# Decode attention with a mixer: keys and values of two neighbouring heads loaded together, in rows of 64 KB

## The chip, the cores and the metric

The kernel runs on one core of one Trainium2 chip. The metric is the device time of one execution in microseconds (us); lower is better. A run of the kernel before is compared with runs of the kernel after on the same chip.

The engines are PE (TensorE, matmuls), DVE (VectorE), ACT (ScalarE), POOL (GpSimd) and SP (SyncE, which here only issues DMA transfers). Each engine works through its own instructions strictly in order. The bytes are moved by 16 DMA engines which all serve one queue of transfers that SP issues.

## What is computed

```python
B, Sq, D = 8, 1, 512
Hq, Hkv, Sk, Dh = 32, 8, 8192, 128
q = (xn @ wq).reshape(B, Sq, Hq, Dh).transpose(0, 2, 1, 3)
scores = einsum("bhqd,bhkd->bhqk", q, repeat(k_cache, 4)) * Dh ** -0.5
o = einsum("bhqk,bhkd->bhqd", softmax(scores), repeat(v_cache, 4))
attention = o.transpose(0, 2, 1, 3).reshape(B, Sq, Hq * Dh) @ wo
# mixer on the second layer norm h of x, token by token
u = gelu(einsum("bsd,sf->bdf", h, w1) + b1)          # F = 1792
return x + attention + (einsum("bdf,fs->bds", u, w2) + b2).transpose(0, 2, 1)
```

One token of 8 batch elements attends to a cache of 8192 positions, with 32 query heads on 8 heads of keys and values. Everything is float32. Keys and values of one head and one batch element are 4 MB each, 537 MB in all: the kernel reads each byte once.

## The kernel before

**Items.** The work is cut into 64 items (`N_IT`), one for each head `h` and batch element `b`, with `h, b = divmod(i, B)`. An item has K(i) and V(i) of 4 MB. Both are loaded with 128 partitions; partition p holds 64 consecutive positions, so one row is 32 KB.

**The ring.** `slots` (in the trace `raw`) is a ring of `RING = 5` slots of 4 MB. `slot()` (L49) hands them out in turn. `load_next()` (L87) takes the next load from the list `order` (K0, K1, V0, K2, V1, ...) and has SP issue it. SP waits with it until the work that last used this slot is done, and everything that SP has to issue later waits behind it. `load_next()` is called where a slot comes free: at the end of `qk(i)` for the keys, and at the end of `pv(i, 1)` for the values.

**What one item needs**, by engine:
- `turn_keys(i, c)` (L256), four times: DVE transposes a chunk of 128 x 2048 keys in place, in blocks of 32 x 32.
- `qk(i)` (L263): PE multiplies 4 blocks of 32 head dimensions with 4 chunks, 16 instructions that add up in one bank `acc`. The queries lie spread out in `z` (`Z`), which `q_place(h)` fills once for each head by matmuls of PE and copies of ACT. [...] The four chunks use four different groups of 32 columns of the array.
- The softmax: `sm_max` (DVE, L282), `sm_spread` (PE, L287, which lays the maxima of all partitions side by side), `sm_bias` (DVE, L293, the maximum over partitions with `hmask`), `sm_exp` (ACT, L304, with a table load ahead of it), `sm_send` (PE, L311, which reorders the partitions with `send`), `sm_turn` (DVE, L322, into one of two tiles `pt`).
- `pv(i, part)` (L327): PE multiplies with V, 16 instructions in two parts. `o_take` (ACT, L358) copies the result to `ob`, and `o_place` (after every fourth item) sums and scales it with `ohg`, `pick` and `keep` into `ot`. `o_project(h)` (L402) multiplies a whole head with `wo`, and `load_wo` loads the next 1 MB of `wo` afterwards.

**The order.** It is written by hand (`manual_schedule`), in `pair(i)` (L439): one turn of the loop handles three items at different stages, i the transposition of keys, i-1 the QK and softmax, i-2 the PV. The last items have an order of their own (from L493 on), and in the last fifteen turns SP also issues a tiny transfer into `pad` (L490).

**The mixer** is spread between. It has 112 pieces `mx_step(b, j)` (14 for each of 8 batch elements, two in each turn): a gelu on ACT, a product and a sum on POOL. Where one batch element ends, `mx_end(b)` (L431) has PE sum `macc` over partitions (L433) and DVE add the result to `yrow` (L434), and `mx_begin` has PE spread the next row into `hb` (L419).

Of the kernel before, what the change touches and what calls it, by code (L numbers as in the profile page):

```python
# [10 lines left out]
ALU = mybir.AluOpType  # L11
# [17 lines left out]
N_IT = B * HKV  # L29
RB = 2 * REP  # L30
# [10 lines left out]
def attn_mixer_kernel(ctx: ExitStack, tc: tile.TileContext, x, kc, vc, wq, wo, w1, b1, w2, b2, out):  # L41
# [29 lines left out]
    KR, VR = {}, {}  # L71
    order = []
    for i in range(N_IT):
        order.append((2 * i, kc, KR, i))
        order.append((2 * (i + LAG) + 1, vc, VR, i))
# [10 lines left out]

    def load_next():  # L87
        if order:
# [4 lines left out]
            first, last = to is KR and not i, not order  # L93
            at = 0
            for n in (CH_T,) * NCH if first else PIECES if last else (NT,):
                nc.sync.dma_start(t[:, at:at + n, :], rows[:, at:at + n, :])
                at += n
# [6 lines left out]
    def load_wo(h):  # L104
        t = place.tile([P, REP, D], F32, name="wo")
        how = "(r p) n -> p r n" if h == HKV - 1 else "(p r) n -> p r n"
        rows = wo[h * REP * DH:(h + 1) * REP * DH, :].rearrange(how, p=P)
# [10 lines left out]
    w1t = const.tile([P, NF], F32, name="w1t")  # L118
    b1t = const.tile([P, NF], F32, name="b1t")
    w2t = const.tile([P, NF], F32, name="w2t")  # L120
    b2t = const.tile([B, 1], F32, name="b2t")
    yrow = const.tile([W, D], F32, name="yrow")
    for _ in range(RING - 2):
        load_next()
# [12 lines left out]
    oh = early[:, 3, W:W + REP]  # L137
    nc.vector.tensor_reduce(oh, ident.rearrange("p (g h) -> p h g", h=REP), AX.X, ALU.add)
    ohw = early[:, 2, :P]
    nc.vector.tensor_copy(ohw.rearrange("p (g h) -> p g h", h=REP),  # L140
                          oh.unsqueeze(1).to_broadcast([P, P // REP, REP]))
    hmask = const.tile([P, P], F32, name="hmask")
    nc.vector.tensor_scalar(hmask, ohw, 1.0, 3.0e38, op0=ALU.subtract, op1=ALU.mult)
    oh32 = early[:, 3, :W]
    nc.vector.tensor_reduce(oh32, ident.rearrange("p (j x) -> p x j", x=W), AX.X, ALU.add)
    ohu = const.tile([P, GT * REP], F32, name="ohu")
    nc.vector.tensor_copy(ohu, oh32[:, :GT * REP])
# [8 lines left out]
    ohg = const.tile([P, P], F32, name="ohg")  # L156
    nc.vector.tensor_scalar(ohg.rearrange("p (h g) -> p h g", h=REP), oh.unsqueeze(2).to_broadcast([P, REP, W]),
                            lmask, None, op0=ALU.mult)
    send = const.tile([P, P], F32, name="send")
    nc.vector.tensor_copy(send.rearrange("p (x c h) -> p c x h", c=NCH, h=REP),  # L160
                          ident.rearrange("p (c x h) -> p c x h", c=NCH, h=REP))
# [4 lines left out]
    pick = const.tile([P, GT, P], F32, name="pick")  # L166
    nc.vector.tensor_copy(pick.rearrange("p u (h g) -> p (u h) g", h=REP),
                          ohu.unsqueeze(2).to_broadcast([P, GT * REP, W]))
    keep = const.tile([P, P], F32, name="keep")
    nc.vector.tensor_copy(keep.rearrange("p (g c) -> p g c", c=REP), oh32.unsqueeze(2).to_broadcast([P, W, REP]))  # L170
# [9 lines left out]
    Z = const.tile([P, NB, B, W], F32, name="z")  # L180
# [43 lines left out]
    def q_project():  # L224
# [16 lines left out]
        load_next()  # L241

    def q_place(h):
        m = misc()
        for q in range(NB):
            nc.tensor.matmul(m[:, q * B * REP:(q + 1) * B * REP], rep[:, q, :], QT[:, h].rearrange("p b r -> p (b r)"),
                             start=True, stop=True)
        src = m[:, :NB * B * REP].rearrange("p (x r) -> p x r", r=REP)
        dst = Z.rearrange("p q b (a k r) -> p (q b) a k r", k=2, r=REP)
        for a in range(NB):  # L250
            x = slice(a * W, (a + 1) * W)
            for k in range(2):
                nc.scalar.copy(dst[x, :, a, k, :], src[x])
# [9 lines left out]
    def qk(i, part=None):  # L263
# [4 lines left out]
        for q in range(NB):  # L268
            for c in range(NCH) if part is None else range(part * NCH // 2, (part + 1) * NCH // 2):
                nc.tensor.matmul(S[i][c * W:(c + 1) * W, :].rearrange("p (t j) -> p t j", j=W),  # L270
                                 Z[:, q, b, :], k[:, c * CH_T:(c + 1) * CH_T, q * W:(q + 1) * W],
# [37 lines left out]
    def sm_send(i):  # L309
        m = misc()  # L310
        nc.tensor.matmul(m, send, st[i][0], start=True, stop=True)  # L311
# [41 lines left out]
    def o_take(i):  # L353
# [7 lines left out]
        oc = one.tile([P, DH], F32, name=f"oc{i % 2}")  # L361
# [11 lines left out]
    def o_place(i):  # L373
# [3 lines left out]
        if h < HKV - 1:  # L377
            if b % HB < HB - 1:
                return
            ob = OB.pop(h)  # L380
            m = misc()
            nc.tensor.matmul(m[:, :HB], ohg, LR.pop(i // HB), start=True, stop=True)
            rl = work.tile([P, HB], F32, name="rl4")
            nc.vector.reciprocal(rl, m[:, :HB])
            m = misc()
            for c in range(NCH):
                nc.tensor.matmul(m.rearrange("p (b d) -> p b d", b=HB), pick[:, c, :], ob[:, :, c * DH:(c + 1) * DH],  # L387
                                 start=(c == 0), stop=(c == NCH - 1))
            t = big()
            nc.vector.tensor_tensor(t.rearrange("p (b d) -> p b d", b=HB), m.rearrange("p (b d) -> p b d", b=HB),  # L390
                                    keep.unsqueeze(1).to_broadcast([P, HB, P]), op=ALU.mult)
            s = work.tile([P, HB, REP], F32, name="s4")
            nc.vector.tensor_reduce(s, t.rearrange("p (b g c) -> p b c g", b=HB, c=REP), AX.X, ALU.add)
            o = b - HB + 1
# [187 lines left out]
```

## Time and profile before

| | us |
|---|---|
| three runs | 1294.78, 1294.83 (median), 1295.08 |
| the profiled execution | 1294.88 |
| its span, first to last instruction | 1293.1 |
| PE, DVE, ACT, POOL busy | 829.3, 726.9, 331.2, 229.6 |
| bytes moved by DMA | 554.45 MB, mean 429 GB/s |

All numbers of the trace come from the one profiled execution. Its rows are read so: in a row of the timeline stand the start, the length, the engine, the line, the operation with output and inputs, how many were merged (x), and in brackets the idle time of the engine ahead of it with what ended it. In a row of a group stand the busy time in all, the mean of one in ns, and the idle time ahead of it. In a row of stretches stand the length, the busy time of PE, PE's weight loads, DVE, ACT and POOL, then the granted clock of TensorE (1.00 is full speed), the mean busy share of the DMA engines and what they moved in GB/s. The share of a short stretch can be over 1, since a packet is counted where it begins.

### The profile page before, as it was taken

Reading aid. Unit: us, or ns where it says so; the run is one execution under the profiler, and the core shown is the slowest. Engines: PE = TensorE matmul, PEld = TensorE weight load, DVE = VectorE, ACT = ScalarE, POOL = GpSimd, SP = SyncE. Lnnn points to the kernel's source line nnn. Section 1 sums busy time; section 2 is a strip of 40 time slices with the busy share of each in tenths; the row PEclk is TensorE's granted clock in tenths of the full one; section 3 lists DMA queues with packets and bytes.
Section 4 is the critical chain, followed back from the end, with each engine's and each line's share of the span. In section 5 each row is a group of like instructions: output and inputs, shape, how many; then the busy total and the mean of one; then the engine's idle time right before and its main releaser. Section 6 shows DMA issues by size and latency. Waiting matters only on the chain.

```text
span 1293.1 us, 11759 instructions
## 1 busy us (share of the span) xinstructions
PE 829.3 (64%) x4890; PEld 244.5 (19%) x4890; DVE 726.9 (56%) x648; ACT 331.2 (26%) x479; POOL 229.6 (18%) x247
## 2 busy tenths in 40 slices
PE   2664766756757656666657576567564774657777
PEld 0111211211211111211112111121121221112223
DVE  2655456565555554654646556556456555556774
ACT  0232323222422313223233132232323232311000
POOL 1112112211212122121121131211211221110000
PEclk9877778878878788787887797787876887878899
DMA  9999999999999999999999999999999999999997
GB/s 407 426 432 436 430 435 432 432 432 434 431 432 433 433 432 431 436 431 430 434 431 433 433 430 435 431 433 433 432 431 431 435 432 428 435 432 430 433 437 315
DMA packets 21640, 554.45 MB, mean 429 GB/s; under 512 B 2732, under 2 KB 2764, under 8 KB 3540
## 3 DMA queue, kind: packets, MB, share of 16 engines
q1 hardware_dynamic: 21444, 553.68, 99.4%
q8 instruction: 38, 0.62, 0.2%
q14 instruction: 14, 0.11, 0.0%
q0 software_dynamic: 128, 0.02, 0.0%
q10 hardware_dynamic: 16, 0.02, 0.0%
HBM read 553.69 MB, written 0.02 MB: 428 GB/s over the span
## 4 chain that ended last, share of the span: by engine, by line
DMA 66%; PE 19%; DVE 14%; issue 1%; ACT 0%; SPq 0%; POOL 0%; ACTq 0%; DVEq 0%; POOLq 0%
DMA raw<-in_A_k_cache_dram 63%; PE acc L337 13%; DVE raw L259 12%; DMA raw<-in_A_v_cache_dram 2%; PE misc L287 2%; DMA b2t<-in_B_b_dram 2%; DVE mr L282 1%; PE acc L270 1%; PE misc L230 1%; PE misc L433 0%; PE misc L387 0%; PE hb L419 0%; PE misc L311 0%; DVE oc L366 0%; PE misc L218 0%
## 5 line engine op out<-in xcount | busy, mean ns | idle before, releaser
L259 DVE STREAM_TRANSPOSE raw<-raw 128x2048 f32<-128x2048 f32 x256 | 583.6, 2295 | 292.1 <-DMA raw<-in_A_k_cache_dram 292.1
L337 PE MATMUL acc<-raw,pt 128*32 128x512 f32 x2016 | 340.2, 829 | 0.0
L287 PE MATMUL misc<-ident,mr 128*128 128x128 f32 x128 | 47.0, 466 | 401.0 <-DVE mr L282 401.0
L270 PE MATMUL acc<-raw,z 128*32 128x512 f32 x2048 | 261.0, 609 | 9.7 <-DVE raw L259 7.6
L428 POOL TENSOR_SCALAR g<-g,w2t 128x512 f32<-128x512 f32 x112 | 77.7, 694 | 789.7 <-ACT g L427 789.7
L304 ACT ACT_TABLE_LOAD x57 | 73.1, 1283 | 333.8 <-DVE nb L293 333.5
L429 POOL TENSOR_TENSOR macc<-macc,g 128x512 f32<-128x512 f32 x112 | 142.3, 1271 | 9.4
L427 ACT ACTIVATE g<-hb,b1t,w1t 128x512 f32<-128x512 f32 x112 | 87.1, 777 | 219.7 <-PE hb L419 127.1
L322 DVE STREAM_TRANSPOSE pt<-misc 128x512 f32<-128x512 f32 x64 | 45.5, 710 | 140.0 <-PE misc L311 140.0
L337 PEld LDWEIGHTS acc<-raw,pt 128*32 128x32 f32 x2016 | 74.9, 145 | 211.5 <-issue 210.3
L287 PEld LDWEIGHTS misc<-ident,mr 128*128 128x128 f32 x128 | 29.4, 285 | 449.3 <-DVE mr L282 449.3
L304 ACT ACTIVATE t2k<-acc,nb 128x512 f32<-128x512 f32 x64 | 44.0, 688 | 233.4 <-DVE nb L293 232.8
L270 PEld LDWEIGHTS acc<-raw,z 128*32 128x32 f32 x2048 | 66.5, 111 | 186.3 <-issue 169.7
L311 PE MATMUL misc<-t2k,send 128*128 128x512 f32 x128 | 76.0, 677 | 23.4 <-ACT t2k L304 23.4
L427 ACT ACT_TABLE_LOAD x57 | 73.1, 1283 | 1.0
L358 ACT COPY ob<-acc 128x512 f32<-128x512 f32 x56 | 32.7, 584 | 98.9 <-PE acc L337 98.9
L387 PE MATMUL misc<-ob,pick 128*128 128x512 f32 x112 | 51.5, 603 | 0.0
L282 DVE TENSOR_REDUCE mr<-acc 128x1 f32<-128x512 f32 x64 | 41.8, 653 | 3.0 <-PE acc L270 3.0
L311 PEld LDWEIGHTS misc<-t2k,send 128*128 128x128 f32 x128 | 19.4, 191 | 78.4 <-issue 40.7
L434 DVE TENSOR_TENSOR yrow<-misc,yrow 32x512 f32<-32x512 f32 x8 | 5.4, 678 | 42.7 <-PE misc L433 42.7
L405 PE MATMUL misc<-wo,ot 128*32 128x512 f32 x56 | 27.0, 629 | 0.0
L421 POOL MEMSET macc<- 128x512 f32 x8 | 4.2, 525 | 116.4 <-PE misc L433 97.2
(90 smaller groups left out, 229.5 us busy)
## 6 DMA issues: line engine op xcount, KB each, us to landing
raw<-in_A_k_cache_dram SPq DMA_DIRECT2D x63, 4096.0 KB
raw<-in_A_v_cache_dram SPq DMA_DIRECT2D x63, 4096.0 KB
wo<-in_A_wo_dram SPq DMA_DIRECT2D x7, 1024.0 KB
raw<-in_A_k_cache_dram SPq DMA_DIRECT2D x4, 1024.0 KB
raw<-in_A_v_cache_dram SPq DMA_DIRECT2D x3, 1024.0 KB
raw<-in_A_v_cache_dram SPq DMA_DIRECT2D x2, 512.0 KB
wo<-in_A_wo_dram SPq DMA_DIRECT2D x4, 256.0 KB
ob<-in_A_x_dram ACTq DMA_DIRECT2D x1, 16.0 KB
```

Source lines behind the costliest of these rows:

```text
L259: nc.vector.transpose(k, k)
L270: nc.tensor.matmul(S[i][c * W:(c + 1) * W, :].rearrange("p (t j) -> p t j", j=W), Z[:, q, b, :], k[:, c * CH_T:(c + 1) * CH_T, q * W:(q + ...
L282: nc.vector.tensor_reduce(mr, S[i], AX.X, ALU.max)
L287: nc.tensor.matmul(m[:, :P], st[i].to_broadcast([P, P]), ident, start=True, stop=True)
L304: nc.scalar.activation(p, S.pop(i), AF.Exp, bias=st[i], scale=SCALE, accum_out=lr)
L311: nc.tensor.matmul(m, send, st[i][0], start=True, stop=True)
L322: nc.vector.transpose(PT[i % NPT][:, :CH_T * W], st.pop(i)[0])
L337: nc.tensor.matmul(O[i][j * W:(j + 1) * W, :].rearrange("p (c d) -> p c d", c=NCH), pt[:, t * W:(t + 1) * W], v[:, t], start=(t < NB), sto ...
L387: nc.tensor.matmul(m.rearrange("p (b d) -> p b d", b=HB), pick[:, c, :], ob[:, :, c * DH:(c + 1) * DH], start=(c == 0), stop=(c == NCH - 1))
L427: nc.scalar.activation(g, hb, AF.Gelu_apprx_tanh, bias=b1t[:, j:j + 1], scale=w1t[:, j:j + 1])
L428: nc.gpsimd.tensor_scalar(g, g, w2t[:, j:j + 1], 1.0, op0=ALU.mult, op1=ALU.mult)
L429: nc.gpsimd.tensor_add(acc, acc, g)
```

## The change

The first six heads (`PAIRED = 6`) are handled two at a time, in 24 steps (`N_PR`), one for each pair of heads `g` and batch element `b`. The last two heads stay with `pair(i)`, whose loop now starts at item `FIRST = 48`.

**Loads.** The keys of two neighbouring heads lie behind each other in DRAM. One load of 8 MB takes both: the first head in partitions 0 to 63, the second in 64 to 127, with 128 consecutive positions (64 KB) in each partition. It takes two neighbouring slots of the ring. Where only the last slot of the ring is left before it wraps, which is so for every fifth load, it becomes two loads of 4 MB and rows of 32 KB (V0, K3, V5, K8, V10, K13, V15, K18, V20, K23). The order is K0, V0, K1, V1, ...; in step i K(i+1) is issued after the first half of K(i), and V(i+1) after the first half of V(i).

**The step.** Its keys are transposed in eight chunks and multiplied in four quarters of two chunks, all of which add up in one bank (`Z` is wider by four columns, and the two halves take it at different offsets). Then there is one softmax for both heads, with one exponential and two sends, and the PV in two halves. The steps do not overlap as the items did: transposition, QK, softmax and PV of one step follow each other in the order of the program. Four pieces of the mixer (`mix(1)`) stand behind the four quarters.

**The rest.** The masks `hmask`, `send`, `ohg`, `pick` and `keep` exist in two forms: `fill_softmax(True, ...)` and `fill_place(True, ...)` write those for pairs at the start, and the calls with `False` in `pair(48)` write the others. Three small vectors moved into `pad`; the fifteen tiny transfers of the last turns are gone.

```diff
+    duo = [(src, to, i) for i in range(N_PR) for src, to in ((kc, KP), (vc, VP))][::-1]
+
+    def load_duo():
+        src, to, i = duo.pop()
+        g, b = divmod(i, B)
+        rows = src[b, 2 * g:2 * g + 2].rearrange("h (p t) d -> (h p) (t d)", p=HP)
+        half = NT * DH
+        if taken[0] % RING < RING - 1:
+            t = slot(2).rearrange("p s m -> p (s m)")
+            n = 1 if to is VP or i else 4
+            for a in range(n):
+                x = slice(a * 2 * half // n, (a + 1) * 2 * half // n)
+                nc.sync.dma_start(t[:, x], rows[:, x])
+            parts = [t[:, k * half:(k + 1) * half] for k in range(2)]
+        else:
+            parts = []
+            for k in range(2):
+                t = slot().rearrange("p s m -> p (s m)")
+                nc.sync.dma_start(t, rows[:, k * half:(k + 1) * half])
+                parts.append(t)
...
     def load_next():
-        if order:
+        if duo:
+            load_duo()
+        elif order:
...
+    def qk_duo(i, k, cs):
...
+        for q in range(NB):
+            for c in cs:
+                nc.tensor.matmul(SD[i][c * W:(c + 1) * W, :].rearrange("p (t j) -> p t j", j=W),
+                                 Z[:, q, b, (1 - k) * REP:(1 - k) * REP + W],
+                                 t[:, c * CH_T:(c + 1) * CH_T, q * W:(q + 1) * W],
+                                 start=(not k and not q), stop=(k == 1 and q == NB - 1))
+
+    def softmax_duo(i):
...
+        nc.vector.tensor_reduce(mr, s, AX.X, ALU.max)
+        m = misc()
+        nc.tensor.matmul(m[:, :P], mr.to_broadcast([P, P]), ident, start=True, stop=True)
...
+        nc.scalar.activation(p, s, AF.Exp, bias=nb, scale=SCALE, accum_out=LD[i // HB][:, b % HB:b % HB + 1])
+        for k in range(2):
+            m = misc()
+            nc.tensor.matmul(m, send[:, k, :], p, start=True, stop=True)
+            nc.vector.transpose(PT[k][:, :CH_T * W], m)
...
+    def mix(n):
+        for _ in range(n):
+            b, j = divmod(step[0], NF)
+            step[0] += 1
+            if j == 0 and 0 < b <= B:
+                mx_end(b - 1)
+            if b < B:
+                if j == 0:
+                    mx_begin(b)
+                mx_step(b, j)
...
+    def duo_step(i):
+        g, b = divmod(i, B)
+        half = NCH // 2
+        for k in range(2):
+            for x in range(2):
+                for c in range(half):
+                    turn_duo(i, k * NCH + x * half + c)
+                qk_duo(i, k, range(x * half, (x + 1) * half))
+                mix(1)
+            if not k:
+                load_next()
+                if i == N_PR - 1:
+                    load_next()
+        if i == N_PR - 1:
+            load_next()
+        del KP[i]
+        softmax_duo(i)
+        if b == B - 1 and g < PAIRED // 2 - 1:
+            q_place_duo(g + 1)
+        pv_duo(i, 0)
+        load_next()
+        if i:
+            place_duo(i - 1)
...
+        pv_duo(i, 1)
+        if i == N_PR - 1:
+            load_next()
+        del VP[i]
+        take_duo(i)
...
-    spare = pad[:16, :60].rearrange("p (n k) -> p n k", k=4)
-    for i in range(N_IT - 2):
+    for i in range(FIRST, N_IT - 2):
         pair(i)
-        n = N_IT - 3 - i
-        if 0 < n < 16:
-            nc.sync.dma_start(spare[:n, n - 1, :], wo[:n, :4])
```

What this does to the order of the instructions shows at the places where the mixer passes from one batch element to the next. On PE this was so before, in the turn that has the QK of item 7, the last of the first head (L270 is QK, L246 `q_place`, L287 and L311 the softmax, L337 the PV, L433 `mx_end`, L419 `mx_begin`):

```order
L270 MATMUL acc<-raw,z 32x512 x16
L246 MATMUL misc<-qt,rep 128x32 x4
L287 MATMUL misc<-ident,mr 128x128
L337 MATMUL acc<-raw,pt_146 32x512 x8
L433 MATMUL misc<-macc,bsel 32x512
L419 MATMUL hb<-hn,ident 128x512
L337 MATMUL acc<-raw,pt_146 32x512 x8
L311 MATMUL misc<-t2k,send 128x512
```

And this is PE now in step 7, where the mixer passes to its third element (L491 is `qk_duo`, L580 `mx_end`, L566 `mx_begin`, L502 and L511 the softmax, L328 `q_place_duo`, L523 `pv_duo`):

```order
L491 MATMUL acc<-raw,z 32x512 x8
L580 MATMUL misc<-macc,bsel 32x512
L566 MATMUL hb<-hn,ident 128x512
L491 MATMUL acc<-raw,z 32x512 x24
L502 MATMUL misc<-ident,mr 128x128
L511 MATMUL misc<-t2k,send 128x512 x2
L328 MATMUL misc<-qt,rep 64x32 x8
L523 MATMUL acc<-raw,pt_156 32x512 x16
L523 MATMUL acc<-raw,pt_158 32x512 x16
```

The matmul of `mx_end` stood between two halves of the PV of an earlier item; now it stands between the first and the second quarter of the step's QK, and the PV of the same step comes after the whole QK, the softmax and the two sends.

On DVE the same place read so before (L259 is the transposition of a chunk of keys, L282 and L293 the softmax, L434 the addition of `mx_end`, L322 the transposition into `pt`):

```order
L259 STREAM_TRANSPOSE raw<-raw 128x2048 x2
L282 TENSOR_REDUCE mr<-acc 128x1
L434 TENSOR_TENSOR yrow<-misc,yrow 32x512
L259 STREAM_TRANSPOSE raw<-raw 128x2048
L293 ISA t2k,nb<-misc,hmask 128x128
L293 ISA nb 128x1
L259 STREAM_TRANSPOSE raw<-raw 128x2048
L322 STREAM_TRANSPOSE pt_148<-misc 128x512
```

And now, in step 7 (L480 is the transposition of keys, L581 the addition, L500 and L504 the softmax, L512 the transpositions into `pt`):

```order
L480 STREAM_TRANSPOSE raw<-raw 128x2048 x2
L581 TENSOR_TENSOR yrow<-misc,yrow 32x512
L480 STREAM_TRANSPOSE raw<-raw 128x2048 x6
L500 TENSOR_REDUCE mr<-acc 128x1
L504 ISA t2k,nb<-misc,hmask 128x128
L504 ISA nb 128x1
L512 STREAM_TRANSPOSE pt_156<-misc 128x512
L512 STREAM_TRANSPOSE pt_158<-misc 128x512
```

The addition stood between the maximum of an item and the transposition of the third chunk of keys of the next item; now it stands between the second and the third of eight transpositions of keys whose QK, softmax and PV all come later in the same step.

More of the change, by code (lines that the diff above doesn't have):

```diff
@@ L29 @@
 N_IT = B * HKV
+PAIRED = 6
+N_PR = PAIRED // 2 * B
+FIRST = PAIRED * B
+ZW = W + REP
 RB = 2 * REP
@@ L92, in load_next @@
             rows = src[b, h].rearrange("(p t) d -> p t d", p=P)
-            first, last = to is KR and not i, not order
+            last = not order
             at = 0
-            for n in (CH_T,) * NCH if first else PIECES if last else (NT,):
+            for n in PIECES if last else (NT,):
                 nc.sync.dma_start(t[:, at:at + n, :], rows[:, at:at + n, :])
@@ L310, in sm_send @@
         m = misc()
-        nc.tensor.matmul(m, send, st[i][0], start=True, stop=True)
+        nc.tensor.matmul(m, send[:, 0, :], st[i][0], start=True, stop=True)
         st[i] = (m, st[i][1])
@@ new lines, in attn_mixer_kernel, with pv_duo @@
+    LD, OD, OBD = {}, {}, {}
+    def pv_duo(i, k):
+        b = i % B
+        if not k:
+            OD[i] = ps_a.tile([P, 512], F32, name="acc")
+        v = VP[i][k].rearrange("p (c t) d -> p t c d", c=NCH)
+        for t in range(CH_T):
+            j = t % NB
+            nc.tensor.matmul(OD[i][j * W:(j + 1) * W, :].rearrange("p (c d) -> p c d", c=NCH),
+                             PT[k][:, t * W:(t + 1) * W], v[:, t],
+                             start=(not k and t < NB), stop=(k == 1 and t >= CH_T - NB))
@@ L477, in pair @@
             sm_turn(k)
-        if mixing:
-            mx_step(mb, mj + 1)
-        if b == 3 and h:
+        if step[0] <= B * NF:
+            mix(1)
+        if h == PAIRED and b == 1:
+            o_project(h - 2)
+            load_wo(h - 1)
+        if b == 3:
             o_project(h - 1)
```

233 lines of the change are left out of this document (160 added, 73 removed).

## The prediction

> **What bounds the kernel now.** I read the stretches of the trace first: for each stretch its length, the busy time of five engines (with counts), the granted TensorE clock, the busy share of the DMA engines and GB/s.
>
> ```profile
> 60.00:1200.00 1140.00, 727.67 (x4190) 211.06 (x4186) 637.97 (x535) 315.61 (x447) 220.27 (x228) 0.80 1.00 432
> 7.35:17.07 9.72, 0.61 (x4) 0.55 (x4) 4.55 (x19) 0.59 (x2) 0.00 (x0) 1.00 1.00 433
> ```
>
> From 60 to 1200 us the DMA engines are busy all the time (1.00) at 432 GB/s, while the busiest engine, PE, works 728 of 1140 us. A load of one head (4.19 MB) therefore takes 9.7 us, the pair's load (8.39 MB) 19.4 us, and nothing on an engine counts unless it lets this queue run dry. So the next view is the chain that ended last, which shows how far ahead of its need a load is issued.
>
> ```profile
> 133.41 28.95 DMA raw<-in_A_k_cache_dram
> 174.43 26.67 DMA raw<-in_A_k_cache_dram
> ```
>
> A K load lands 26.7 to 29.0 us after its issue, of which its own bytes need 9.7: the queue holds 17 to 19 us of other work when it is issued. That is the reserve of before: an engine's delay of 10 us costs nothing. The wait that releases such an issue is mostly PV, as the waits of the DMA queue show (us in total, times, longest).
>
> ```profile
> SPq L96 <- PE acc L337: 828.4, 61, 20.8
> ```
>
> **What the change can gain.** (1) The rows. The 7.35 to 17.07 us stretch holds only the load of wq, whose rows are 64 KB like the new ones: 433 GB/s against 432 with 32 KB rows. The 48 pair loads last 48 x 19.4 = 931 us; by the two rows the gain is 0.23%, 2.1 us, but 432 is a mean with small loads in it, so the bounds are 0 and 2.1 and I take 1. The Trainium skill (DMA: Bandwidth & Descriptors, "Why small descriptors are slow") gives each packet a fixed cost of about 3 cycles on top of one cycle per 32 bytes; by that rule half as many packets would save 3 of 2054 cycles, an estimate of 1.4 us, and the sum would be 0.4 us lower. (2) Fewer small transfers and one maximum, bias and exponential for two heads: all beside a saturated queue, 0. What hides them is the DMA time itself. (3) The setup has some 20 more small DVE operations, and the masks are filled again at the seventh head. The first lie ahead of a wait for b2t,
>
> ```profile
> 23.10 0.47 DVE L210 TENSOR_SCALAR macc<-ob,b2t 8x512 f32<-8x512 f32 x1 [10.20 <-DMA b2t<-in_B_b_dram]
> ```
>
> which leaves 10.2 us of cover; the second (about 3 us of DVE) stand where 4 MB loads again lie in the queue: 0. Without that cover they would cost these 3 us once.
>
> **What it can lose.** The ring still has five slots of 4 MB, but a load now takes two. In step i K(i+1) may be issued when the first half of K(i) is multiplied (the second half of V(i-1) is by then), V(i+1) when the first half of V(i) is, which stands behind the whole softmax of step i. I set time 0 at the first transposition of K(i), which comes when K(i) has landed. V(i) lands at 19.4, K(i+1) at 38.8. The queue stays full only if K(i+1) is issued a lead before 19.4 and V(i+1) a lead before 38.8. The lead (from issue to landing without the bytes) is bounded by the one small transfer that finds the queue empty:
>
> ```profile
> 1290.06 0.66 SPq L553 DMA_DIRECT2D out_dram<-macc  x1
> SPq L578 <- DMA out_dram<-macc: 1.1, 1, 1.1
> ```
>
> 1.8 us (0.66 and 1.1) at least, 3.0 (to the end of the span at 1293.1) at most; I take 2.4. So the deadlines are 17.0 and 36.4. Now the chain of an ordinary step, with these rows (start, us, engine, line, operation, idle before):
>
> ```profile
> 162.37 4.50 DVE L259 STREAM_TRANSPOSE raw<-raw 128x2048 f32<-128x2048 f32 x2 [3.39 <-DMA raw<-in_A_k_cache_dram]
> 1263.12 3.63 PE L270 MATMUL acc<-raw,z 128*32 128x512 f32 x16
> 1261.99 0.65 DVE L282 TENSOR_REDUCE mr<-acc 128x1 f32<-128x512 f32 x1
> 1262.70 0.49 PE L287 MATMUL misc<-ident,mr 128*128 128x128 f32 x2 [1.34 <-DVE mr L282]
> 169.59 0.25 DVE L293 CUSTOM_DVE_ANT_0 t2k<-misc,hmask 128x128 f32<-128x128 f32 x1
> 169.94 1.28 ACT L304 ACT_TABLE_LOAD   x1 [7.00 <-DVE nb L293]
> 171.82 0.19 ACT L304 ACTIVATION_READ_ACCUMULATOR t2k<-acc,nb 128x1 f32 x1
> 174.28 1.12 PE L311 MATMUL misc<-t2k,send 128*128 128x512 f32 x2
> 56.29 2.08 PE L311 MATMUL misc<-t2k,send 128*128 128x512 f32 x2 [3.02 <-ACT t2k L304]
> 1248.36 1.92 PE L337 MATMUL acc<-raw,pt 128*32 128x512 f32 x16
> 150.93 6.24 PE L337 MATMUL acc<-raw,pt 128*32 128x512 f32 x32
> 54.00:58.00 4.00, 1.71 (x2) 0.50 (x2) 2.31 (x3) 3.88 (x6) 1.96 (x2) 0.50 0.97 418
> ```
>
> - Eight transpositions at 2.25 end at 4.5, 9.0, 13.5 and 18.0 by pairs. QK comes in quarters of two chunks each (8 instructions, 16 in the trace): 3.63 at full clock, as the same shape in the tail shows, no less than the whole four chunks take, since two chunks fill only half of the array's columns.
> - After 3 us of idleness PE has a granted clock of 0.50 (last row), and the same send takes 2.08 instead of 1.12. Before the first quarter PE has been idle some 5 us, so this quarter takes 3.63 to 7.3; I take 5.5. The quarters end at 10.0, 13.6, 17.2, and (from 18.0) 21.6. K(i+1) is issued at 13.6, 3.4 before its deadline.
> - Maximum to the end of its spreading 1.2 (22.8), bias 0.4 (23.2), table load, exponential and accumulator read 2.2 (25.4), two sends 2.2 to 4.2, middle 3.2 (28.6), first half of PV, 32 in the trace: 3.8 (twice 1.92) to 6.2, middle 5.0 (33.6). V(i+1) is issued at 33.6 (31.4 to 35.9), 2.8 before its deadline. An ordinary step loses nothing, but the reserve has shrunk from 17 us to under 3.
>
> Five steps are not ordinary. Where the mixer passes to its next batch element (once in 14 of its pieces, four pieces a step: steps 3, 7, 10, 14, 17, 21), DVE has an addition that waits for a matmul which PE has behind the quarter just issued. Before the change it looks so:
>
> ```profile
> 190.66 1.02 PE L433 MATMUL misc<-macc,bsel 128*32 128x512 f32 x2
> L434 DVE TENSOR_TENSOR yrow<-misc,yrow 32x512 f32<-32x512 f32 x8 | 5.4, 678 | 42.7 <-PE misc L433 42.7
> 37.43 0.98 PE L246 MATMUL misc<-qt,rep 128*128 128x32 f32 x8
> ```
>
> Eight times DVE stood still 5.3 us and nobody paid. Now, as the rows of DVE and PE in the section on the change show, the rest of the key transpositions is queued behind it, then the last quarter, the softmax, PV, and SP with the next load.
>
> - Steps 10 and 17 (after the third quarter): that quarter ends at 17.2, mixer matmul 18.2, addition 19.0 instead of 13.5; last transposition 23.5, last quarter 27.1 instead of 21.6. V is issued at 33.6 + 5.5 = 39.1, 2.7 late, twice: 5.4 us.
> - Step 7 (after the first quarter): addition at 11.8 instead of 4.5, so 7.3 later, and the queries of the next pair (twice the row of 0.98, half-width, I take 1.0) stand in front of PV: V at 41.9, 5.5 late. K(8) is one of the loads that the ring's end splits in two, whose first half is issued early: nothing lost there.
> - Steps 14 and 21 (after the first quarter): the second pair of transpositions ends at 11.8 + 4.5 = 16.3, its quarter at 19.9: K is issued 2.9 after its deadline, twice 5.8. In step 21 V is late by another 40.9 - 39.3 = 1.6 (its deadline has moved by 2.9); in 14 V(15) is split.
> - Step 3 has K(3) split, so it begins up to 9.7 early: 0.
>
> Sum: 5.4 + 5.5 + 5.8 + 1.6 = 18.3 lost, 1 gained: +17.3. Steps 0 to 2 take over the slots of wq and have the same chain (V(0) is split, K(0) comes in four pieces); the tail is unchanged in order, and the 15 tiny transfers taken out of it are issued by SP while it waits: 0. The profiled execution took 1294.88 us (span 1293.1, 1.8 around it), the median shown is 1294.83; 1294.9 + 17.3 = 1312.2.
>
> Bounds of the sum. Low ends of all (lead 1.8, PE at full clock, V at 31.4): step 10 issues at 36.9 against 37.0, step 7 loses 0.8, steps 14 and 21 (18.0 against 17.6) 0.4 each: 1.6. High ends (lead 3.0, V at 35.9, half clock): 5.6 in steps 10 and 17 each, 11 in step 7, 6.3 in 14 and 21 each, 0.1 in some 11 ordinary steps: 36. So 1294 to 1331.
>
> **Rivals.**
> - *Every step late.* If the chain of an ordinary step is longer than 36.4, each of about 11 unsplit ordinary steps loses the excess, and the five others too. For it: only 2.8 us of reserve, and place_duo and o_project delay DVE's next step by up to 2 us. At 1.5 over the deadline (4.3 more than the sum has): 16.5 + 18.3 + 5 x 4.3 = 56, 1350; at 0.5 over, 5.5 + 18.3 + 16.5 = 40, 1334. Against it: the high end of the rows is 35.9.
> - *Rows win (the other side).* The 64 KB rows run at the rate of the best 50 us stretches, 435 GB/s, instead of 432: place, the pair loads; price, 0.7% of 931 = 6.4 us gained. It decides where the loss is under 6.4, so with the low ends: 1294.9 + 1.6 - 6.4 = 1290.
>
> ```profile
> 50.00:100.00 50.00, 30.84 (x175) 8.17 (x174) 27.88 (x23) 16.65 (x21) 12.47 (x14) 0.80 1.01 435
> 100.00:120.00 20.00, 11.08 (x68) 2.97 (x68) 10.43 (x8) 5.48 (x7) 4.02 (x5) 0.74 0.98 420
> ```
>
>   Against it: that stretch has 32 KB rows and share 1.01, so it is the edge of a window, and wq shows 433.
> - *Rows lose.* The halves of a pair load lie 4 MB apart in DRAM, twice as far as before, and neighbouring rows 64 KB. If that made the reads collide, all pair loads would run at, say, the lowest 20 us row, 420: 931 x 12/420 = 27 us more, and more time for the engines, so nothing else is late: 1322. Against it: wq has the same layout and runs at 433. The Trainium skill (DMA: Bandwidth & Descriptors, "Latency and other measured facts") says that row pitches of large powers of two slow copies, 3% at 512 KiB and half at 4 MiB; by that rule this rival would come, and the wq row does not agree.
> - *The change doesn't do what it says*: a fifth of the loads stay two loads of 32 KB rows, by the ring's end; this is in the sum.
>
> **How the numbers follow.** Chances: the sum as it stands, some five late loads, 0.64 (1302 to 1325); every step late 0.12; rows lose 0.04; rows win, or nothing is late, 0.20 (1289 to 1301), of which 0.10 is faster by more than 0.2% (2.6 us, what a measurement of this kernel can tell from no change), 0.07 within it, 0.03 a little slower. So faster 0.10, same 0.07, slower 0.83. The range leaves out the fastest tenth and most of "every step late": 1295 to 1331.
>
> **What would show it.** Right: DMA share under 1 in about five 20 us stretches (steps 7, 10, 14, 17, 21, near 350, 475, 620, 755, 900 us) and 1.00 between them; DVE's wait for the mixer's matmul of 5 us or more, and the next K or V issue late behind it. V issued 32 to 35 us after the first transposition in other steps. Wrong: share 1.00 throughout, or gaps in each step, or a busy share of 1.00 with another GB/s than 432 (then it is the rows). If the two sends and PV run at full clock after the exponential, the reserve is 5 us and half of the loss is gone.

## The result and the profile after

The changed kernel took 1306.39 us (median of 5 runs, 1304.63 to 1308.19), the kernel before 1294.90 (5 runs, 1294.78 to 1295.54): 0.87% slower, ratio 1.0087 with a 95% interval of 1.0076 to 1.0099. The profiled execution took 1306.54 us, its span is 1304.6. Two executions in the device's slower state, one of e11 (1581.22 us) and one of the kernel before beside e9 to e12 (3823.88), are left out of the ratios further on.

The stretches of the changed kernel come first (length, busy time of PE, weight loads, DVE, ACT and POOL with counts, granted clock, DMA share, GB/s): the long middle, the stretch up to 340 us, the five places that the prediction named, and three stretches between them.

```profile
60.00:1200.00 1140.00, 832.99 (x4032) 222.27 (x4034) 606.48 (x450) 215.87 (x295) 216.25 (x224) 0.86 0.99 427
60.00:340.00 280.00, 199.84 (x944) 51.07 (x944) 143.65 (x97) 49.27 (x63) 56.67 (x59) 0.85 1.00 433
...
340.00:380.00 40.00, 31.60 (x174) 9.40 (x174) 22.13 (x18) 10.12 (x16) 7.85 (x8) 0.93 0.97 413
460.00:480.00 20.00, 16.67 (x88) 4.90 (x85) 5.50 (x8) 2.06 (x3) 0.05 (x1) 0.91 0.99 424
600.00:640.00 40.00, 30.62 (x137) 8.04 (x136) 16.89 (x13) 8.98 (x11) 8.37 (x9) 0.84 0.88 375
740.00:780.00 40.00, 33.54 (x158) 8.70 (x154) 21.66 (x17) 6.42 (x9) 9.28 (x10) 0.97 1.00 422
860.00:920.00 60.00, 48.85 (x228) 13.21 (x224) 25.36 (x24) 9.29 (x13) 8.38 (x9) 0.86 0.94 396
380.00:460.00 80.00, 61.05 (x276) 15.63 (x270) 41.64 (x29) 12.01 (x15) 16.14 (x17) 0.85 1.00 433
500.00:600.00 100.00, 71.85 (x350) 18.84 (x348) 47.95 (x37) 16.72 (x22) 15.69 (x16) 0.86 1.00 432
640.00:740.00 100.00, 77.00 (x350) 20.10 (x352) 60.80 (x40) 18.16 (x27) 22.67 (x24) 0.88 1.00 433
```

In the stretches shown outside the five places the queue is as full as before, at 432 to 433 GB/s. At the five it falls short: 40 us at 375 instead of 433 are 40 x (1 - 375/433) = 5.4 us lost (step 14), 60 us at 396 are 5.1 (step 21), 40 us at 413 are 1.9 (step 7), 40 at 422 are 1.0 (step 17), 20 at 424 are 0.4 (step 10; the 40 us from 460 on have 436 GB/s, so this one may be an effect of the window's edge). Together 13.8, where this execution is 11.7 longer than that of before (1306.54 against 1294.88); most of the 2 between them is what the rows gain (e4).

How one such place comes about stands in the chain that ended last (start, us, what). The chain around step 14:

```profile
569.91 26.17 DMA raw<-in_A_k_cache_dram
...
596.10 4.52 DVE raw L480 x2
600.62 0.04 issue
600.66 4.22 PE acc L491 x13
...
605.39 0.68 DVE yrow L581
606.07 4.42 DVE raw L480 x2
610.49 0.04 issue
610.54 6.54 PE acc L491 x17
617.08 0.02 issue
617.10 22.95 DMA raw<-in_A_k_cache_dram
```

Two transpositions, the first quarter, then the mixer's addition (L581) between the transpositions, then the second pair and the second quarter, and only then the load of K(15), 21.0 us after the first transposition. Just ahead of that second quarter PE stood still for 1.98 and 1.15 us, with two matmuls between, since DVE came to these transpositions late. The granted clock of that second quarter and of one us inside it:

```profile
610.50:617.10 6.60, 6.56 (x23) 1.85 (x25) 6.60 (x4) 2.05 (x3) 4.09 (x5) 0.55 0.37 159
615.00:616.00 1.00, 1.00 (x10) 0.40 (x6) 1.00 (x1) 0.00 (x0) 0.92 (x2) 0.50 0.00 0
```

The DMA engines stand still while PE multiplies at half clock (0.50). The share of 0.00 alone would not show it, since a packet is counted where it begins; but by the packets of the trace the last ones in the queue began at 612.6 and took 2.4 us, so the engines are idle from 615.1 until the first packet of K(15) begins at 618.1. DVE's wait for the mixer's matmul (us in total, times, longest) is even shorter than before, where it was 42.7, 8 times; what changed is that it is now paid for:

```profile
DVE yrow L581 <- PE misc L580: 31.6, 8, 5.8
```

### The profile page after: what moved, and what is told of

Read it like the earlier page. It is cut to its first block, busy times and chain, and to the rows that moved or that the text cites. A ratio compares the mean times of both kernels' runs of the same rounds, so it can differ in the third digit from the quotient of the medians.

```text
span 1304.6 us, 11227 instructions
## 1 busy us (share of the span) xinstructions
PE 945.8 (72%) x4782; PEld 259.4 (20%) x4782; DVE 701.1 (54%) x581; ACT 229.0 (18%) x321; POOL 229.6 (18%) x247
## 4 chain that ended last, share of the span: by engine, by line
DMA 53%; PE 24%; DVE 21%; ACT 1%; issue 1%; POOL 0%; DVEq 0%; ACTq 0%; POOLq 0%
DMA raw<-in_A_k_cache_dram 49%; DVE raw L480 16%; PE acc L491 12%; PE acc L523 3%; DVE raw L336 3%; PE acc L414 3%; PE misc L511 2%; DMA raw<-in_A_v_cache_dram 2%; DMA b2t<-in_B_b_dram 2%; PE misc L540 1%; PE acc L347 1%; DMA wo<-in_A_wo_dram 1%; PE misc L297 1%; ACT L508 1%; PE misc L468 1%
## 5 line engine op out<-in xcount | busy, mean ns | idle before, releaser
L491 PE MATMUL acc<-raw,z 128*32 128x512 f32 x1536 | 405.0, 663 | 161.3 <-DVE raw L480 158.0
L480 DVE STREAM_TRANSPOSE raw<-raw 128x2048 f32<-128x2048 f32 x192 | 424.5, 2272 | 144.1 <-DMA raw<-in_A_k_cache_dram 144.1
L575 POOL TENSOR_SCALAR g<-g,pad 128x512 f32<-128x512 f32 x112 | 77.4, 691 | 742.5 <-ACT g L574 742.5
L491 PEld LDWEIGHTS acc<-raw,z 128*32 128x32 f32 x1536 | 95.0, 119 | 469.0 <-issue 292.4
L523 PE MATMUL acc<-raw,pt 128*32 128x512 f32 x1536 | 188.0, 631 | 0.0
L574 ACT ACTIVATE g<-hb,pad 128x512 f32<-128x512 f32 x112 | 87.0, 777 | 214.1 <-POOL macc L576 165.5
L511 PE MATMUL misc<-t2k,send 128*128 128x512 f32 x96 | 76.7, 944 | 56.5 <-ACT t2k L508 56.5
L512 DVE STREAM_TRANSPOSE pt<-misc 128x512 f32<-128x512 f32 x48 | 34.4, 717 | 106.7 <-PE misc L511 106.2
L347 PE MATMUL acc<-raw,z 128*32 128x512 f32 x512 | 80.6, 626 | 10.3 <-DVE raw L336 8.1
L523 PEld LDWEIGHTS acc<-raw,pt 128*32 128x32 f32 x1536 | 47.8, 116 | 144.8 <-issue 114.1
L414 PE MATMUL acc<-raw,pt 128*32 128x512 f32 x480 | 76.5, 776 | 0.0
L500 DVE TENSOR_REDUCE mr<-acc 128x1 f32<-128x512 f32 x24 | 16.6, 691 | 92.5 <-PE acc L491 92.5
L364 PE MATMUL misc<-ident,mr 128*128 128x128 f32 x32 | 10.6, 424 | 74.9 <-DVE mr L359 74.9
L531 ACT COPY ob<-acc 128x512 f32<-128x512 f32 x24 | 14.0, 585 | 285.5 <-PE acc L523 285.5
L511 PEld LDWEIGHTS misc<-t2k,send 128*128 128x128 f32 x96 | 23.0, 263 | 79.9 <-ACT t2k L508 61.1
L381 ACT ACTIVATE t2k<-acc,nb 128x512 f32<-128x512 f32 x16 | 11.0, 687 | 135.8 <-DVE nb L370 135.7
L347 PEld LDWEIGHTS acc<-raw,z 128*32 128x32 f32 x512 | 18.9, 113 | 60.9 <-issue 41.7
```

What stands on the lines that cost most here:

```text
L414: nc.tensor.matmul(O[i][j * W:(j + 1) * W, :].rearrange("p (c d) -> p c d", c=NCH), pt[:, t * W:(t + 1) * W], v[:, t], start=(t < NB), sto ...
L480: nc.vector.transpose(k, k)
L491: nc.tensor.matmul(SD[i][c * W:(c + 1) * W, :].rearrange("p (t j) -> p t j", j=W), Z[:, q, b, (1 - k) * REP:(1 - k) * REP + W], t[:, c * C ...
L511: nc.tensor.matmul(m, send[:, k, :], p, start=True, stop=True)
L512: nc.vector.transpose(PT[k][:, :CH_T * W], m)
L523: nc.tensor.matmul(OD[i][j * W:(j + 1) * W, :].rearrange("p (c d) -> p c d", c=NCH), PT[k][:, t * W:(t + 1) * W], v[:, t], start=(not k an ...
```

## The experiments

Theory T: the time is lost where the mixer's addition stands ahead of key transpositions and makes the next load late, and nowhere else. Rivals: the loss lies in the rows, in the refilled masks or in the longer step as such; or the mixer's other work holds the step up; or the order on DVE is harmless without PE's half clock. No kernel leaves work out; each ratio is to runs of the kernel before on the same chip, with its 95% interval.

**e1, e2, e3, e9, e10: the mixer's pieces behind the V load.** In the steps listed, the pieces from the batch element's end on are issued behind the first half of PV and the load of V. e1 lists all six steps, e2 (14, 21), e3 (7, 10, 17), e9 all but 7, e10 all but 10 and 17.

```diff
                 qk_duo(i, k, range(x * half, (x + 1) * half))
-                mix(1)
+                if i in (3, 7, 10, 14, 17, 21) and (late or step[0] % NF == 0):
+                    late += 1
+                else:
+                    mix(1)
...
         pv_duo(i, 0)
         load_next()
+        mix(late)
```

> In the six steps in which the mixer passes to its next batch element, its pieces from the passing on are issued behind the first half of PV and the V load, not behind a key quarter. Theory (the time is lost only where the mixer's addition holds back key transpositions): the loss of 11.5 us goes, 1295 us (1293.5 to 1296.5), and the trace shows DMA share 1.00 at 432 to 434 GB/s at 340-380, 600-640 and 860-920 us, where it was 0.97, 0.88 and about 0.9. Rival (the loss comes from the rows, the setup, the second filling of the masks or the longer step as such): 1303 to 1307, little changed.

Measured: 1293.42 us (11 runs, 1292.94 to 1294.62), ratio 0.9988 (0.9980 to 0.9997): the whole loss is gone, and the kernel is a little faster than the one before. The same step and the same stretches in e1:

```profile
593.76 4.52 DVE raw L480 x2
598.27 0.04 issue
598.32 8.02 PE acc L491 x32
606.34 0.02 issue
606.36 27.21 DMA raw<-in_A_k_cache_dram
```

```profile
600.00:640.00 40.00, 28.75 (x142) 7.13 (x140) 20.86 (x15) 6.42 (x9) 9.12 (x11) 0.93 1.00 432
860.00:920.00 60.00, 47.50 (x236) 12.15 (x236) 33.32 (x26) 7.79 (x11) 10.44 (x12) 0.89 1.01 435
```

K is issued 12.6 us after the first transposition (8.4 earlier than in the changed kernel) and takes 27.2 to land, since it waits behind the loads that are still in the queue. T holds; setup, masks and the longer step cost nothing that shows.

> The same edit in steps 14 and 21 alone (late K loads). From the trace of the changed kernel: 40 us at 375 GB/s (600-640) and at 386 (860-900) against 433 in the undisturbed stretches are 5.4 and 4.4 us lost, so 1306.4 - 9.8 = 1296.6 (1295 to 1298.5). By the sizes of the prediction's sum (7.4 of 18.3 in these steps) only 4.7 of the 11.5 would go: 1301.7. If the steps don't add up (a late K load only moves the next loss), 1300 or more.

Measured: 1299.83 (12 runs, 1296.58 to 1304.93), ratio 1.0038 (1.0026 to 1.0051). That lies between the two forecasts, 1296.6 by the windows and 1301.7 by the prediction's sizes. Against e1, what is left in steps 7, 10 and 17 costs 6.4 us, twice what the windows of one execution gave (3.3). The spread of 8.3 us, where e1 has 1.7, says why one execution is not enough here.

> The same edit in steps 7, 10 and 17 alone (late V loads). From the trace of the changed kernel: 40 us at 413 GB/s (340-380), 436 (460-500), 422 (740-780) against 433 are 1.9, 0 and 1.0 us lost, so 1306.4 - 2.9 = 1303.5 (1302 to 1305). By the sizes of the prediction's sum (10.9 of 18.3 in these steps) 6.9 would go: 1299.5.

Measured: 1300.14 (5 runs, 1298.47 to 1301.83), ratio 1.0038 (1.0026 to 1.0050). That is near the 1299.5 of the prediction's sizes and not the 1303.5 of the windows. What is left, steps 14 and 21, costs 6.7 us against e1, where the windows gave 10.5. 6.4 and 6.7 are 13.1, and the changed kernel stands 13.0 above e1: the two kinds of steps add up.

> As e1, but step 7 as in the changed kernel (its mixer's addition ahead of six key transpositions). By the prediction's sum this step costs 5.5 us: 1298.9. By the traces (V issued 36.4 to 39.3 us after the first transposition, against a deadline of about 36): 0.5 to 3.5, 1294 to 1297.

Measured: 1296.68 (11 runs, 1295.48 to 1298.51), ratio 1.0013 (1.0005 to 1.0022): step 7 costs 3.3 us, at the high end of what the traces gave and well under the 5.5 of the sum.

> As e1, but steps 10 and 17 as in the changed kernel (the addition ahead of the last two key transpositions). By the prediction's sum 2.7 us each: 1298.8. By the traces (V issued 35.5 to 41.0, the late ones where the last quarter and the sends run at half the granted clock): 0 to 5 each, and a spread of several us from run to run where e1 has 1.7: 1295 to 1300.

Measured: 1297.06 (8 runs, 1294.59 to 1299.91), ratio 1.0020 (1.0010 to 1.0030): 3.6 us for both steps, with a spread of 5.3. DVE's maximum in step 10, in the trace of the changed kernel and then in that of e10 (in brackets its wait for the last quarter):

```profile
462.46 0.69 DVE L500 TENSOR_REDUCE mr<-acc 128x1 f32<-128x512 f32 x1 [4.27 <-PE acc L491]
```

```profile
462.75 0.69 DVE L500 TENSOR_REDUCE mr<-acc 128x1 f32<-128x512 f32 x1 [6.64 <-PE acc L491]
```

The order of the instructions is the same in both; the quarter came 2.4 us later in e10, where its granted clock was low (0.53 at 455 to 460 us), and the queue then ran dry:

```profile
455.00:460.00 5.00, 3.85 (x11) 0.92 (x12) 1.10 (x1) 0.78 (x1) 1.97 (x3) 0.53 1.03 447
470.00:475.00 5.00, 5.00 (x34) 1.30 (x34) 0.72 (x1) 0.00 (x0) 0.00 (x0) 0.77 0.29 121
```

**e11: the addition alone.** The two mixer matmuls, its activations and products stay where the changed kernel has them.

```diff
-        nc.vector.tensor_add(yrow, m[:W, :], yrow)
+        owed.append(m)
...
+    def mx_add():
+        if owed:
+            nc.vector.tensor_add(yrow, owed.pop()[:W, :], yrow)
...
         nc.vector.tensor_tensor_reduce(big()[:, :P], m[:, :P], hmask, -SCALE, 3.0e38, ALU.add, ALU.min, nb)
+        mx_add()
```

> The changed kernel with one thing moved: the mixer's addition on DVE stands behind the bias of the step's softmax, where DVE waits for the exponential. The mixer's matmuls, exponentials and products stay where the changed kernel has them. If the addition in front of the transpositions is the cause: as e1, 1293.4 (1292.9 to 1294.6). If the mixer's two matmuls on PE or its work on ACT hold the step up: 1300 or more.

Measured: 1293.81 (11 runs, ten of them 1293.27 to 1294.38), ratio 0.9992 (0.9983 to 1.0001). One DVE instruction of 0.68 us, moved in six steps, removes the whole loss: what cost the time is its place, ahead of key transpositions. The mixer's work on PE and ACT is not part of it.

**e4: the rows.** e1, with every pair load but K(0) as two loads of 4 MB.

```diff
-        if taken[0] % RING < RING - 1:
+        if to is KP and not i:
             t = slot(2).rearrange("p s m -> p (s m)")
```

> As e1, but every pair load as two loads of 4 MB with 32 KB rows (the same bytes in the same slots). Where nothing is late, the queue's rate alone sets the time. If rows of 64 KB and 32 KB run alike: equal to e1 within 0.7 us. If 64 KB rows gain what the prediction took (1 to 2.1 us), e4 is that much slower than e1; by the rival 'rows win' 6.4 slower. If 64 KB rows lose, e4 is faster than e1.

Measured: 1295.07 (11 runs, 1294.89 to 1297.10), ratio 1.0002 (0.9993 to 1.0010), 1.65 us above e1. The packets of e1 and of e4, from their pages:

```profile
DMA packets 15925, 554.41 MB, mean 429 GB/s; under 512 B 1884, under 2 KB 1916, under 8 KB 2692
```

```profile
DMA packets 21253, 554.42 MB, mean 429 GB/s; under 512 B 2476, under 2 KB 2508, under 8 KB 3284
```

The same bytes in 5328 packets fewer: 64 KB rows gain 1.65 us, and e4 without them stands where the kernel before stands. (e4 also has two loads in place of one, with 592 packets of under 512 bytes more; the two effects are not separated.) The Trainium skill (DMA: Bandwidth & Descriptors, "Why small descriptors are slow") has a fixed cost of about 3 cycles for each packet, from which the prediction's estimate was 1.4 us; the two runs agree with it. The Trainium skill's row on pitches of large powers of two (the same page, "Latency and other measured facts"), on which the prediction's third rival drew, has figures from 512 KiB on. In both e1 and e4 the rows of neighbouring partitions lie 64 KB apart, so it has no figure for these loads. A pitch of 64 KB instead of 32 costs nothing that shows: e4 has 1295.07, the kernel before 1294.98.

**e6, e7, e12: the reserve of an ordinary step.** Half of the last key chunk (e6), or all of it (e7), is transposed three times instead of once, with the same result: by the time of a whole chunk 2.25 or 4.5 us more on DVE in pair steps 1 to 23 of e1 (e6's dose takes 2.53 in its trace). e12 puts e6's dose into the kernel before, in 46 heads.

```diff
         nc.vector.transpose(k, k)
+        if i and c == 2 * NCH - 1:
+            for _ in range(2):
+                nc.vector.transpose(k[:, :CH_T * DH // 2], k[:, :CH_T * DH // 2])
```

> e1 (no late step), with 2.25 us more on DVE ahead of the last quarter in every pair step but the first (half of the last chunk is turned three times instead of once, with the same result). It measures the reserve of an ordinary step's V load, issued 29.6 to 34.2 us after the first transposition in e1. With the prediction's deadline of 36.4: nothing or next to nothing lost, 1293.4 to 1295. If the deadline lies at 34 or before: 1300 or more.

> As e6 with 4.5 us more (the last chunk is turned three times). V is issued at 34.1 to 38.7. With a deadline of 36.4 the middle of them is 0.5 late and the last 2.3, in some 15 steps whose V load is not split: 5 to 15 us lost, 1298 to 1308. If there is more reserve than the prediction had (over 7 us): 1293.4 to 1295. If less: 1315 or more.

> The kernel before with e6's dose, 2.25 us more of transposition on DVE ahead of the multiplication of the keys, in 46 heads (twice as often as in e6). With 17 to 19 us in the queue at each issue nothing is lost: 1294.9 (1294.3 to 1296). If the reserve of before is no larger than that of e6's kernel, which lost 18 us with half of the doses: 1313 or more.

Measured: e6 1311.39 (4 runs, 1307.91 to 1316.17), ratio 1.0118 (1.0102 to 1.0133); e7 1342.48 (4 runs, 1341.43 to 1343.45), ratio 1.0367 (1.0352 to 1.0381); e12 1294.96 (11 runs, 1294.65 to 1295.60), ratio 1.0001 (0.9992 to 1.0010). In the kernel before, twice as many doses cost nothing; here 18.0 us and 49.1 us over e1. For both e6 and e7 the forecast from the prediction's deadline of 36.4 was too low, and the branch for an earlier deadline came. In e6 the delay has grown when it reaches the load. One of its steps, whose first transposition is at 82.31: the last quarter on PE, then DVE's maximum, then SP's issue of V:

```profile
102.59 5.12 PE L494 MATMUL acc<-raw,z 128*32 128x512 f32 x14 [3.33 <-DVE raw L483]
```

```profile
107.75 0.69 DVE L503 TENSOR_REDUCE mr<-acc 128x1 f32<-128x512 f32 x1 [5.21 <-PE acc L494]
```

```profile
118.79 0.33 SPq L105 DMA_DIRECT2D raw<-in_A_v_cache_dram  x1
```

PE waited 3.33 us ahead of the quarter instead of 0.77, and the quarter took 5.1 instead of 3.6. So V goes out 36.5 us after the first transposition, where e1 had 32.4 in this step: 4.1 later for a dose of 2.53.

**e5, e8: PE kept busy.** Spare matmuls, whose result nobody reads, in the changed kernel: three ahead of the second quarter in steps 14 and 21 (e5), two ahead of the sends in steps 7, 10 and 17 (e8).

```diff
...
                 mix(1)
+                if i in (14, 21) and not k and not x:
+                    warm(3)
```

> The changed kernel, with three spare matmuls of 128x512 on PE behind the mixer's matmuls in steps 14 and 21, so that PE doesn't stand idle ahead of the second quarter. In the trace of the changed kernel that quarter took 6.6 us at a granted clock of 0.55 in step 14 and K was issued 21.0 us after the first transposition. If the clock makes the size of the loss: quarter 3.6 to 4 us, K issued at about 18, and of the 6.6 us that steps 14 and 21 cost (1306.4 against 1299.8 with their addition moved) two thirds or more go: 1300 to 1302.5. If only the order of DVE counts: 1306 (1305 to 1307.5).

> The changed kernel, with two spare matmuls of 128x512 on PE behind the spreading of the maximum in steps 7, 10 and 17, so that PE doesn't stand idle ahead of the sends. In the trace of the changed kernel V was issued 11.1 us after the start of the maximum in step 10 (sends 3.66 us, clock 0.55) and 8.2 us after it in step 17 (sends 1.98, clock 1.00). If the clock makes the size: V 8 to 9 us after the maximum in all three, and most of the 6.3 us of these steps go: 1300 to 1303. If only the order counts: 1306 (1305 to 1307.5).

Measured: e5 1305.23 (5 runs, 1303.63 to 1306.10), ratio 1.0078 (1.0065 to 1.0090); e8 1305.54 (4 runs, 1303.81 to 1307.33), ratio 1.0082 (1.0068 to 1.0095). Both stand about 1 us below the changed kernel, where 3 to 6 were expected, and their intervals overlap its own (1.0076 to 1.0099). Yet in the edited places it went as meant. Step 14 of e5 in its chain, and three of its stretches:

```profile
616.21 3.63 PE acc L491 x16
619.85 0.02 issue
619.87 23.06 DMA raw<-in_A_k_cache_dram
```

```profile
600.00:640.00 40.00, 31.03 (x120) 7.88 (x124) 20.79 (x14) 6.46 (x8) 8.39 (x9) 0.84 0.93 397
860.00:920.00 60.00, 49.06 (x241) 13.85 (x238) 26.86 (x25) 9.22 (x13) 8.40 (x9) 0.97 0.97 414
460.00:500.00 40.00, 33.90 (x142) 8.50 (x142) 20.31 (x14) 7.05 (x9) 9.52 (x10) 0.84 0.88 375
```

The quarter takes 3.63 instead of 6.54, K goes out 18.9 us after the first transposition (at 601.02), and steps 14 and 21 lose 3.3 and 2.6 us instead of 5.4 and 5.1. But in this execution step 10, which lies ahead of the edit, lost 5.4 (375 GB/s in 40 us), where the changed kernel's had lost 0.4. In e8 the sends took 1.98 in steps 7 and 10 instead of 3.40 and 3.66. So in these traces the late load goes out earlier where PE's clock is kept up, but the medians don't show it at the size expected; with 4 or 5 runs, and a spread of several us from steps that the edit doesn't touch, how much the clock is worth stays open. It is no cure: the order on DVE is (e11).

## Why the prediction was right, point by point

- *Forecast.* 1312.2 (1295 to 1331), slower at 0.83; measured 1306.4. The mechanism was right, its size 17.3 instead of 11.5.
- *What bounds the kernel.* Right. Where nothing is late the queue runs at 432 to 433 GB/s after the change too, and the reserve is gone: e12's doses are free, e6's are not.
- *Gain from the rows.* 1 taken (0 to 2.1); measured 1.65 (e4 against e1).
- *Setup, masks, small transfers: 0.* Right: e4, which has all of these and 32 KB rows, stands at 1295.07 against 1294.98.
- *An ordinary step loses nothing.* Right. K was forecast at 13.6 and is issued at 12.6 (e1), the first quarter taking less than the 5.5 forecast; V was forecast at 33.6 (31.4 to 35.9), and in e1 it is 29.5 to 34.2 where V is not split, 32.4 in the step that e6 was compared with. e6 shows how thin the reserve is: with V at 36.5 in the step shown it loses 18 us in all.
- *Five late steps, and step 3 none.* Right as to the places (the windows at 340, 460, 600, 740 and 860 us, and none near 160) and as to the cause (e11). One sign was off: DVE's wait for the mixer's matmul was to be 5 us or more, and is 4.0 in the mean (31.6 in 8) and 5.8 at most.
- *Steps 14 and 21:* 7.4 forecast, 6.7 measured (e3), of parts that were each off and nearly cancel, which is luck. K was to be issued at 19.9 in both. In step 14 of the changed kernel it was 21.0, since the addition ended at 10.0 instead of 11.8 (the first quarter was shorter than the 5.5 forecast), but the second quarter took 6.5 instead of 3.6: the prediction put the half clock at the first quarter of a step and not behind the pause that the addition makes on PE. In step 21 it was 19.8, with a quarter of 6.4 too, but there the first transposition itself came late: `place_duo` of the step before (L550) held DVE until just then, a delay that the prediction named only among its rivals:

```profile
880.56 0.28 DVE L550 TENSOR_TENSOR ot<-s,rl 128x16 f32<-128x16 f32 x2
880.73 4.50 DVE L480 STREAM_TRANSPOSE raw<-raw 128x2048 f32<-128x2048 f32 x2
```

  The further 1.6 for V in step 21 did not come: V was issued at 916.37, 7.4 ahead of the landing of K(22) at 923.73.
- *The lead* was the other part: 1.8 to 3.0 from one store of 16 KB. The K load that found the queue empty took 22.95 from issue to landing, 3.5 more than its own 19.4. So the deadlines are 15.9 and 35.3 instead of 17.0 and 36.4. A load of the pair's size would have given a nearer bound than the small store: that of wq, the first in the queue, takes 22.2 us on the page of the changed kernel, 2.8 more than its bytes.
- *Steps 10 and 17:* 5.4 forecast, 3.6 measured (e10). The forecast treated the two steps alike. But ahead of step 10 SP issues a load of 1 MB of wo as well (at 432.01 us, before K(11)), whose bytes take 2.4 us at 433 GB/s, so that V's deadline is 37.7 there, by 35.3 and 2.4. In the changed kernel's trace V goes out 37.5 us after the first transposition and the 40 us from 460 on lose nothing; in e10's it goes out at 41.0 and the queue runs dry. Besides, the forecast had a middle clock, and the last quarter and the sends ran at full or half clock from one execution to the next. In the changed kernel's trace the sends took, in step 10 and in step 17,

```profile
466.24 3.66 PE L511 MATMUL misc<-t2k,send 128*128 128x512 f32 x4 [2.54 <-ACT t2k L508]
...
747.38 1.98 PE L511 MATMUL misc<-t2k,send 128*128 128x512 f32 x4 [1.31 <-ACT t2k L508]
```

  the first after a pause of 2.54 us, the second after 1.31, with a granted clock of

```profile
466.50:470.00 3.50, 3.50 (x8) 1.07 (x12) 0.78 (x2) 0.00 (x0) 0.00 (x0) 0.55 0.82 356
748.50:750.50 2.00, 2.00 (x15) 0.46 (x17) 1.43 (x2) 0.00 (x0) 0.00 (x0) 1.00 0.80 344
```

- *Step 7:* 5.5 forecast, 3.3 measured (e9). This is the most mis-sized term. In the changed kernel, where the first transposition is at 316.87, the addition, the queries (from the chain) and SP's issue of V stand so:

```profile
325.83 0.68 DVE L581 TENSOR_TENSOR yrow<-misc,yrow 32x512 f32<-32x512 f32 x1 [4.45 <-PE misc L580]
```

```profile
350.69 0.59 PE misc L328 x16
```

```profile
354.91 0.33 SPq L105 DMA_DIRECT2D raw<-in_A_v_cache_dram  x1
```

  The addition ends at 9.6 (11.8 forecast), the queries take 0.6 (1.0), and V is issued at 38.0 (41.9), 2.7 past the deadline of 35.3: of the 3.9 us between forecast and trace 2.2 come from the first quarter, which was forecast cold, 0.4 from the queries, and the rest from what follows.
- *Sum.* Forecast 5.5 + 5.4 + 7.4 - 1 = 17.3. Measured 3.3 + 3.6 + 6.7 - 1.65 = 12.0, against 11.5 for the whole change. The bounds, 1.6 and 36, held; the high one leaves out step 21's V, which by the same high ends (V some 10 later, its deadline 6.3 later) would add about 4.
- *Rivals.* "Every step late" did not come, but was near: some 2.5 us on DVE bring it about (e6). "Rows win" had its sign right and a quarter of its price, 1.65 of 6.4; with e1's order it decides. "Rows lose" fell with e1, which reads these rows and is faster than the kernel before. The pitch that the prediction cites for it is the distance of neighbouring rows, and that is 64 KB here; the two halves, 4 MB apart, lie one behind the other.

## What to carry to other kernels

When loads are made twice as large in a ring of the same size, look not at the rate but at the reserve: how long after a slot's last reader the next load must be on its way, and which waits of other engines stand in that chain; other loads in the queue (here 1 MB of wo) add to the reserve of single steps. A wait that cost nothing with 17 us of reserve is paid for once the reserve is under 3 us, and with more than its length where PE's clock falls meanwhile. An instruction that waits for another engine belongs behind the instructions that free a slot, in a place where its engine waits anyway; moved there, the change is worth what its rows are worth (1293.4 to 1293.8 us against 1294.9).

## What the runs showed of the hardware beyond what was expected

- A load of 8.4 MB that finds the queue empty takes 22.95 to 23.19 us (the K loads of steps 14 and 21; 23.06 in e5), 3.5 to 3.8 more than its bytes at 433 GB/s; wq at the start, of the same size, took 22.2. Where the next load is issued in time it costs nothing that shows: e1 runs at 432 and 435 GB/s in the two stretches above. Row of step 21:

```profile
900.54 23.19 DMA raw<-in_A_k_cache_dram
```

- The granted clock was 0.55 after a pause of PE of 2.54 us and 1.00 after one of 1.31 (the sends of steps 10 and 17). But the length of the pause does not decide it: in step 18 of the same trace it was 1.00 after 2.54 us (the sends took 1.98), and in step 13 of e1 0.57 after 1.31 (3.34). The last quarter of step 10 ran fast in one execution and slowly in another. The times of a kernel spread over 1.7 us where no load was late (e1) and over 8.3 where V loads were (e2). The Trainium skill (TensorE: Matmul & The Clock Gate, "What's actually happening") has the clock halved after an idle window of about 3.4 us that runs free of the program; that would fit the change from run to run. But a low clock after pauses of 2.54 and 1.31 us, shorter than such a window, goes beyond what the section states (ahead of each stood only 0.49 us of work behind another pause of 0.78), and no run here measures the window itself.
